# Three forms of the same matrix products in the second layer of a token-mixing MLP

## The chip, the cores and the metric

The kernel runs on one core of one Trainium2 chip. The metric is the device time of one execution in microseconds. Beside plain times there is one profiled execution, in which the hardware profiler records each instruction and each transfer. In its answers PE is TensorE's stream of products, PEld is TensorE's weight loads, DVE is VectorE, ACT is ScalarE, POOL is GpSimd, and SP is the queue that issues most transfers. L1401 means line 1401 of the kernel. A product is written weights' rows * weights' columns, then rows x columns of the streamed operand.

## The reference

The input has 2048 tokens of 448 channels. Two blocks follow each other, each with a layer norm, a scale and shift, and a gate from a small modulation product. The first is a state-space convolution along the tokens. The second, which holds the change, is an MLP along the token axis, shared by all channels:

```
h = layernorm(x) * (1 + cb) + sb              # (2048 tokens, 448 channels)
u = gelu(einsum("bsd,sf->bdf", h, w1) + b1)   # 1792 hidden units per channel
y = einsum("bdf,fs->bds", u, w2) + b2         # back to 2048 tokens
out = x + gb * transpose(y)
```

Everything is float32.

## The kernel before

The first 400 us or so compute the convolution with its Fourier transforms; the change doesn't touch them. They hold products that serve as neighbours of the new forms: line 599 multiplies 64 rows on each half of TensorE's array with 512 streamed columns (type F32R, and bf16), line 802 does so with 224 columns in plain float32, line 1212 uses the whole array with 224 columns in plain float32, and line 682 uses four strips of 32 weight columns with 64 streamed columns.

The MLP works with split operands. Each float32 matrix is held as a high part of the type F32R and a low part that is the remainder (tiles whi and wlo for weights, uh and ul for the hidden units, h3h and h3l for the normed input). One float32 product is made of three: high by high, high weights by low data, low weights by high data.

The first layer (`mlp1`, lines 1325 to 1334) runs over the hidden units in two halves of seven blocks of 128, with seven accumulators in PSUM. `gelu` (line 1369) then writes uh and ul for each half, `kh` = 0 and 1.

The second layer (lines 1390 to 1407) runs over 16 blocks `t` of 128 tokens. For each block it takes one accumulator `o` (128 tokens by 448 channels, one of seven PSUM buffers), and for both halves `kh` and the seven `k` in each it issues the three products of 448 columns, at lines 1401, 1402 and 1403: 42 products a block, 672 in all. The eviction is two operations of VectorE: line 1405 adds the bias and multiplies with the gate, line 1406 adds the residual `xt`, which was loaded back from device memory. Line 1407 stores the block.

The weights come through `WeightStream` (lines 166 to 218). It counts 64 parts of 128 rows by 896 columns; part n = 32 + 2t + kh belongs to half kh of block t. Three buffers take the raw parts from memory (line 190), four hold the split ones. `begin` casts a part to whi on ScalarE (line 207), and `rest` subtracts to wlo on VectorE (line 216) and then issues the load of a later raw part. At the products of part n the kernel calls `ahead(n + 4)`, which makes one part each time, and in the second layer this is part n + 2. A part takes the split buffer of the one four before it, so its cast waits until that one's products are done.

The order of instructions on PE, ACT, DVE and POOL is the order of the program. On SP, in the second layer, a planner sets the order. So on VectorE the two evicting operations of block t stand ahead of the splits that `ahead` issues for block t + 1.

Of the kernel before, what the change touches and what calls it, by code (L numbers as in the profile page):

```python
# [11 lines left out]
F32 = mybir.dt.float32  # L12
# [3 lines left out]
ALU = mybir.AluOpType  # L16
# [5 lines left out]
L, D, N, F = 2048, 448, 256, 1792  # L22
P = 128
# [8 lines left out]
DC = 224  # L32
# [4 lines left out]
WAHEAD = 4  # L37
# [122 lines left out]
def token_pair(a, r, g):  # L160

    rows = a.rearrange("(n g h r) d -> g n h (r d)", g=2, h=2, r=16)
    return rows[g, :, :, r * D : (r + 2) * D]
# [58 lines left out]
def tile_adaln_s4d_mixer(ctx, tc, i, out):  # L222
    nc = tc.nc
# [8 lines left out]
    x2_d = dram.tile([L, D], F32, name="x2_d")  # L232

    cp = ctx.enter_context(tc.tile_pool(name="cp", bufs=1))
    mod = [None] * 3 + [cp.tile([P, D], F32, name=f"mod{k}") for k in range(3, 6)]
# [3 lines left out]
    b2 = cp.tile([P, 16], F32, name="b2")  # L239
# [3 lines left out]
    with ExitStack() as es:  # L243
        V, S, G, T = nc.vector, nc.scalar, nc.gpsimd, nc.tensor
# [47 lines left out]
        xt = xp.tile([P, 16, D], F32, name="xt")  # L292
# [201 lines left out]
        rs = xp.tile([P, 16], F32, name="rs")  # L494
# [455 lines left out]
        rows, cols, pieces = iter(range(16)), iter(range(32)), [0, 0]  # L950
# [88 lines left out]
        for s in range(tail):  # L1039
            if s == 32:  # L1040
# [6 lines left out]
                t0 = fp.tile([P, 2, P], F32, name="t0", bufs=1)  # L1047
# [83 lines left out]
            if s > 32:  # L1131
                go = pieces[0] < NP and (s % 2 == 1 or s >= NHALF)
# [15 lines left out]
        wst = WeightStream(tc, ctx, i)  # L1148
# [18 lines left out]
        def ln_load(r, ahead=True):  # L1167
            vts[r] = rot.tile([P, 2, D], F32, tag="vt", name="vt", bufs=4)
            nc.sync.dma_start(vts[r], v_v[r])
            if ahead and r % 2 and 1 < r < 15:  # L1170
                x_pair(r + 1)
# [26 lines left out]
        def ln_y(r):  # L1198
            y = py.tile([P, D], F32, tag="y", name="y")
            vt = vts.pop(r)  # L1200
            for g in range(2):
                T.matmul(y[64 * g : 64 * g + 64], ft, vt[:, g], start=True, stop=True)  # L1202
            return y_sum(r, y)
# [16 lines left out]
        def ln_mod(r):  # L1220
            mean, rs = sa.pop(r)
            h = rot.tile([P, D], F32, tag="h", name="h", bufs=3)
            total = small("sum", "b")
            V.reciprocal(rs, rs)
            V.scalar_tensor_tensor(h, xts[r // 2][:, r % 2], mean, mod[4], ALU.add, ALU.mult)
            V.scalar_tensor_tensor(h, h, rs, mod[3], ALU.mult, ALU.add, accum_out=total)  # L1226
            sb[r] = stats(h, total, "b")
            hs[r] = h

        def ln_out(r):  # L1230
            mean, rs = sb.pop(r)
            h = hs.pop(r)
            V.reciprocal(rs, rs)
            V.tensor_tensor(mean, mean, rs, ALU.mult)
            if r == 0:

                S.activation(h3h[:, r], h, AF.Identity, bias=mean, scale=rs)  # L1237
                exact = rot.tile([P, D], F32, tag="h", name="h", bufs=3)
                V.tensor_scalar(exact, h, rs, mean, ALU.mult, ALU.add)
                V.tensor_tensor(h3l[:, r], exact, h3h[:, r].bitcast(F32), ALU.subtract)  # L1240
                return None
            S.activation(h, h, AF.Identity, bias=mean, scale=rs)  # L1242
            S.copy(h3h[:, r], h)
            return lambda: V.tensor_tensor(h3l[:, r], h, h3h[:, r].bitcast(F32), ALU.subtract)
# [69 lines left out]
    with ExitStack() as es:  # L1314
        es.enter_context(tc.manual_schedule(engines={ENG.PE, ENG.Activation, ENG.DVE, ENG.Pool}))
        V, S, G = nc.vector, nc.scalar, nc.gpsimd
        kp = es.enter_context(tc.tile_pool(name="mk", bufs=1))
        up = es.enter_context(tc.tile_pool(name="mu", bufs=1))
        pacc = es.enter_context(tc.tile_pool(name="pacc", bufs=7, space=PSUM))
        h3h = kp.tile([P, 16, D], F32R, name="h3h")  # L1320
        h3l = kp.tile([P, 16, D], F32R, name="h3l")
        uh = [up.tile([P, 7, D], F32R, name="uh0"), None]
        ul = [up.tile([P, 7, D], F32R, name="ul0"), None]

        def mlp1(acc, n, f0=0, f1=7):
            fh, r = divmod(n, 16)
            hi, lo = wst.parts[n]
            if f1 == 7:
                wst.parts.pop(n)
            for f in range(f0, f1):  # L1330
                fs = slice(f * P, (f + 1) * P)
                nc.tensor.matmul(acc[f], hi[:, fs], h3h[:, r], start=r == 0, stop=False)  # L1332
                nc.tensor.matmul(acc[f], hi[:, fs], h3l[:, r], start=False, stop=False)  # L1333
                nc.tensor.matmul(acc[f], lo[:, fs], h3h[:, r], start=False, stop=r == 15)  # L1334

        first = ExitStack()
        first.enter_context(tc.manual_schedule(engines={ENG.SP}))
        acc = [pacc.tile([P, D], F32, tag="acc", name="acc") for _ in range(7)]
        for t in range(-2, 16):

            part = wst.begin(t + WAHEAD - 1) if t > 0 else None
            last = ln_out(t + 1) if 0 <= t + 1 < 16 else None

            if t == -1:
                second()
            if t == 0:
                part = wst.begin(3)
                mlp1(acc, 0, 0, 4)
                ln_y(3)()
            if t == -1 or 0 < t < 13:  # L1350
                ln_y(t + 3)()
            if 4 <= t + 7 < 16:
                ln_load(t + 7)
            if t < 0:
                wst.load()
            if 1 <= t + 2 < 16:
                ln_mod(t + 2)
            if last:
                last()
            wst.rest(part, V)  # L1360
            if t == 0:
                mlp1(acc, 0, 4, 7)
            elif t > 0:
                mlp1(acc, t)
        first.close()
        e3.close()
        ru = es.enter_context(tc.tile_pool(name="m2r", bufs=3))

        def gelu(acc, fh):
            for f in range(7):  # L1370
                k = 7 * fh + f
                u = ru.tile([P, D], F32, tag="u", name="u")
                S.activation(u, acc[f], AF.Gelu_apprx_tanh, bias=b1[:, k : k + 1])
                V.tensor_copy(uh[fh][:, f], u)
                V.tensor_tensor(ul[fh][:, f], u, uh[fh][:, f].bitcast(F32), ALU.subtract)

        gelu(acc, 0)
        acc = [pacc.tile([P, D], F32, tag="acc", name="acc") for _ in range(7)]
        for r in range(16):
            if r < 8:  # L1380
                for g in range(2):
                    rows = xts[r][64 * g : 64 * g + 64].rearrange("p r d -> p (r d)")
                    nc.sync.dma_start(token_pair(x2_d, 2 * r, g), rows)
            wst.ahead(16 + r + WAHEAD, V)
            mlp1(acc, 16 + r)
        e2.close()
        uh[1] = up.tile([P, 7, D], F32R, name="uh1")
        ul[1] = up.tile([P, 7, D], F32R, name="ul1")
        gelu(acc, 1)
        for t in range(16):  # L1390
            ss = slice(t * P, (t + 1) * P)
            xt = ru.tile([P, D], F32, tag="x2", name="x2")
            nc.sync.dma_start(xt, x2_d[ss])
            o = pacc.tile([P, D], F32, tag="acc", name="o")
            for kh in range(2):
                n = 32 + 2 * t + kh
                wst.ahead(n + WAHEAD, V)
                hi, lo = wst.parts.pop(n)
                for k in range(7):
                    ks = slice(k * P, (k + 1) * P)  # L1400
                    nc.tensor.matmul(o, hi[:, ks], uh[kh][:, k], start=kh == 0 and k == 0, stop=False)  # L1401
                    nc.tensor.matmul(o, hi[:, ks], ul[kh][:, k], start=False, stop=False)  # L1402
                    nc.tensor.matmul(o, lo[:, ks], uh[kh][:, k], start=False, stop=kh == 1 and k == 6)  # L1403
            y = ru.tile([P, D], F32, tag="y", name="y")
            V.scalar_tensor_tensor(y, o, b2[:, t : t + 1], mod[5], ALU.add, ALU.mult)  # L1405
            V.tensor_tensor(y, y, xt, ALU.add)  # L1406
            nc.sync.dma_start(out[0, ss], y)


# [25 lines left out]
```

## Time and profile before

| what | us |
|---|---|
| median of three runs | 693.96 |
| the three runs | 693.78, 693.96, 703.75 |
| profiled execution, device time | 697.46 |
| its span, first to last instruction | 695.5 |
| second layer, first weight load to last product | 556.3 to 690.7 |

The span is 2 us shorter than the device time of the same execution. The page lists busy time of each engine, the chain of work that ended last, the costliest groups of instructions, and the transfers. Products on TensorE overlap: a record's length is how long one product is under way, and the distance between two starts is what each costs in a stream. The mean granted clock of TensorE was 0.961 over the span, and 1.00 in the second layer. Each plain float32 product of the program leaves two records of a product and of a weight load; each F32R product leaves one.

### The profile page before, as it was taken

To read this page: it belongs to the slowest core of one execution; us is meant where nothing else is said; L and a number is where in the kernel's file an instruction comes from. 1 tells how busy PE (TensorE), PEld (TensorE's weight loads), DVE (VectorE), ACT (ScalarE), POOL (GpSimd) and SP (SyncE) were. 2 spreads that over 40 slices of the span, in tenths; PEclk is the share of its full clock that TensorE was granted. 3 is DMA by queue.
4 is the path that set the end of the run, shared out by engine and by line. 5 is a ranking of instruction groups with operands and counts; after the bars stand their busy time and mean duration, and the time that the engine had idled before them with its cause. 6 is when DMAs were issued, how large, how long until landed. Compare 5 with 4: busy or idle time off the path is not lost. (4 is left out here: it accounts for less than half of the span.)

```text
span 695.5 us, 18257 instructions
## 1 busy us (share of the span) xinstructions
PE 621.8 (89%) x7180; PEld 462.8 (67%) x7180; DVE 459.1 (66%) x880; ACT 438.2 (63%) x876; POOL 270.8 (39%) x324
## 2 busy tenths in 40 slices
PE   0759888888988889798889989999999999999997
PEld 0335455545535556565567767778999999999996
DVE  7469899779879679585886578776622354444431
ACT  5937698878978899999964568777422332222220
POOL 6496548429639778988876300000000000000000
PEclk9988979899999899899999999999999999999999
DMA  7795565357896535545348899975673445555640
GB/s 175 203 198 128 176 218 162 120 200 243 252 293 218 169 98 136 152 119 151 90 117 244 270 245 260 245 177 142 178 237 109 144 132 159 159 159 168 167 130 27
DMA packets 103987, 121.14 MB, mean 174 GB/s; under 512 B 12858, under 2 KB 91822, under 8 KB 103774
## 3 DMA queue, kind: packets, MB, share of 16 engines
q1 hardware_dynamic: 102366, 113.11, 56.6%
q0 software_dynamic: 1536, 6.87, 4.6%
q8 instruction: 57, 0.93, 0.6%
q14 instruction: 28, 0.23, 0.1%
HBM read 84.59 MB, written 34.87 MB: 172 GB/s over the span
## 5 line engine op out<-in xcount | busy, mean ns | idle before, releaser
L207 ACT CAST whi<-w 128x896 fp32r<-128x896 f32 x64 | 59.8, 939 | 133.2 <-PE o L1402 84.7
L651 POOL TENSOR_TENSOR G<-mag,gs 128x512 f32<-128x512 f32 x56 | 71.9, 1283 | 75.7 <-ACT gs L647 75.5
L216 DVE TENSOR_TENSOR wlo<-w,whi 128x896 fp32r<-128x896 f32 x64 | 68.0, 1086 | 40.3 <-ACT whi L207 31.0
L1332 PE MATMUL acc<-h3h,whi 128*128 128x448 f32 x224 | 83.4, 373 | 0.9 <-ACT h3h L1237 0.9
L599 PE MATMUL xg<-tab,lph 64*128 64x512 f32 x112 | 65.5, 587 | 19.8 <-issue 7.1
L1333 PE MATMUL acc<-h3l,whi 128*128 128x448 f32 x224 | 82.2, 367 | 0.0
L682 PEld LDWEIGHTS kg<-E,G 128*32 128x32 f32 x3584 | 60.3, 120 | 32.6 <-issue 15.9
L1402 PE MATMUL o<-ul,whi 128*128 128x448 f32 x224 | 81.4, 363 | 0.0
L1401 PE MATMUL o<-uh,whi 128*128 128x448 f32 x224 | 81.2, 363 | 0.0
L1334 PE MATMUL acc<-h3h,wlo 128*128 128x448 f32 x224 | 81.2, 362 | 0.0
L1403 PE MATMUL o<-uh,wlo 128*128 128x448 f32 x224 | 80.7, 360 | 0.0
L682 PE MATMUL kg<-E,G 128*32 128x64 f32 x3584 | 70.5, 236 | 4.3 <-issue 3.5
L599 PE MATMUL xe<-tab,lph 64*128 64x512 f32 x112 | 65.7, 590 | 8.7 <-ACT gs L648 7.0
L652 POOL TENSOR_TENSOR G<-mag,gs 128x512 f32<-128x512 f32 x56 | 71.8, 1282 | 0.0
L1405 DVE SCALAR_TENSOR_TENSOR y<-o,b,mod 128x448 f32<-128x448 f32 x16 | 10.9, 684 | 80.3 <-PE o L1403 80.3
L628 POOL TENSOR_TENSOR m<-mag,w 128x512 f32<-128x512 f32 x56 | 60.3, 1077 | 6.0 <-DVE E L659 1.5
L653 DVE TENSOR_TENSOR E<-m,xe 128x512 f32<-128x512 f32 x56 | 38.1, 681 | 27.2 <-ACT xe L646 23.5
L636 ACT ACTIVATE ab<-xe 128x512 f32<-128x512 f32 x56 | 33.9, 606 | 30.6 <-PE xe L599 22.9
L1332 PEld LDWEIGHTS acc<-h3h,whi 128*128 128x128 f32 x224 | 42.4, 189 | 14.0 <-ACT h L1242 4.2
L599 PE MATMUL xe<-tab,lex 64*128 64x512 f32 x56 | 31.9, 579 | 18.5 <-DMA lex<-wm 16.9
L610 ACT ACTIVATE mag<-xe 128x512 f32<-128x512 f32 x56 | 35.6, 636 | 14.3 <-PE xe L599 5.4
L1334 PEld LDWEIGHTS acc<-h3h,wlo 128*128 128x128 f32 x224 | 42.4, 189 | 3.1
(236 smaller groups left out, 1472.5 us busy)
## 6 DMA issues: line engine op xcount, KB each, us to landing
w<-in_B_w_dram SPq DMA_DIRECT2D x64, 224.0 KB
w<-in_B_w_dram SPq DMA_DIRECT2D x32, 448.0 KB
yu_d<-yt SPq DMA_DIRECT2D x16, 448.0 KB
yi<-yu_d SPq DMA_DIRECT2D x16, 448.0 KB
us_d<-uo SPq DMA_DIRECT2D x16, 448.0 KB
u<-us_d SPq DMA_DIRECT2D x32, 224.0 KB
v_d<-vt SPq DMA_DIRECT2D x32, 224.0 KB
vt<-v_d SPq DMA_DIRECT2D x14, 448.0 KB
```

Source lines behind the costliest of these rows:

```text
L216: eng.tensor_tensor(lo, w, hi.bitcast(F32), ALU.subtract)
L599: T.matmul(out[k], lhs[r], rhs[r], start=start, stop=stop)
L628: G.tensor_tensor(m2, me, w[:, :, None].to_broadcast([P, GD, 32]), ALU.mult)
L651: G.tensor_tensor(Gt[:, 1], mg_, v32(sg), ALU.mult)
L652: G.tensor_tensor(Gt[:, 0], mg_, v32(cg_), ALU.mult)
L682: T.matmul(kgs[g][32 * q : 32 * q + 32, m], Gt[:, c, d], E[:, c, d], start=h == 0 and c == 0 and m == 0, stop=h == 1 and c == 1, skip_grou ...
L1332: nc.tensor.matmul(acc[f], hi[:, fs], h3h[:, r], start=r == 0, stop=False)
L1333: nc.tensor.matmul(acc[f], hi[:, fs], h3l[:, r], start=False, stop=False)
L1334: nc.tensor.matmul(acc[f], lo[:, fs], h3h[:, r], start=False, stop=r == 15)
L1401: nc.tensor.matmul(o, hi[:, ks], uh[kh][:, k], start=kh == 0 and k == 0, stop=False)
L1402: nc.tensor.matmul(o, hi[:, ks], ul[kh][:, k], start=False, stop=False)
L1403: nc.tensor.matmul(o, lo[:, ks], uh[kh][:, k], start=False, stop=kh == 1 and k == 6)
```

## The change

The 16 token blocks no longer have one form. Blocks 2 and 3 split each product into two of 224 columns with the same weights, in two accumulators. Blocks 4 and 5 split each into two of 64 rows, one on each half of the array, with an accumulator for each half; the eviction adds the two. Blocks 10 and 11 are computed together: their four parts of weights are made first, and then the products of the two blocks alternate, each in its own accumulator. The other ten blocks are as before. The arithmetic is that of before; with halves of 64 rows the order of the sums differs.

```diff
-        for t in range(16):
-            ss = slice(t * P, (t + 1) * P)
-            xt = ru.tile([P, D], F32, tag="x2", name="x2")
-            nc.sync.dma_start(xt, x2_d[ss])
-            o = pacc.tile([P, D], F32, tag="acc", name="o")
-            for kh in range(2):
-                n = 32 + 2 * t + kh
-                wst.ahead(n + WAHEAD, V)
-                hi, lo = wst.parts.pop(n)
-                for k in range(7):
-                    ks = slice(k * P, (k + 1) * P)
-                    nc.tensor.matmul(o, hi[:, ks], uh[kh][:, k], start=kh == 0 and k == 0, stop=False)
-                    nc.tensor.matmul(o, hi[:, ks], ul[kh][:, k], start=False, stop=False)
-                    nc.tensor.matmul(o, lo[:, ks], uh[kh][:, k], start=False, stop=kh == 1 and k == 6)
-            y = ru.tile([P, D], F32, tag="y", name="y")
-            V.scalar_tensor_tensor(y, o, b2[:, t : t + 1], mod[5], ALU.add, ALU.mult)
-            V.tensor_tensor(y, y, xt, ALU.add)
-            nc.sync.dma_start(out[0, ss], y)
+        def mlp2(n, t, products):
+            wst.ahead(n + WAHEAD, V)
+            hi, lo = wst.parts.pop(n)
+            kh = n % 2
+            for k in range(7):
+                ks = slice(k * P, (k + 1) * P)
+                first_, last_ = kh == 0 and k == 0, kh == 1 and k == 6
+                products(hi[:, ks], uh[kh][:, k], first_, False)
+                products(hi[:, ks], ul[kh][:, k], False, False)
+                products(lo[:, ks], uh[kh][:, k], False, last_)
+
+        def whole(o):
+            return lambda w, u, start, stop: nc.tensor.matmul(o, w, u, start=start, stop=stop)
+
+        def column_halves(o):
+            def go(w, u, start, stop):
+                for c in range(2):
+                    cs = slice(c * DC, c * DC + DC)
+                    nc.tensor.matmul(o[c][:, 0:DC], w, u[:, cs], start=start, stop=stop)
+
+            return go
+
+        def row_halves(o):
+            def go(w, u, start, stop):
+                for c in range(2):
+                    rs = slice(64 * c, 64 * c + 64)
+                    nc.tensor.matmul(o[c], w[rs], u[rs], start=start, stop=stop)
+
+            return go
+
+        forms = {2: "columns", 3: "columns", 4: "rows", 5: "rows"}
+        for t0 in range(16):
+            if t0 == 11:
+                continue
+            both = (10, 11) if t0 == 10 else (t0,)
+            os_, xs_ = [], []
+            form = forms.get(t0)
+            for t in both:
+                xt = ru.tile([P, D], F32, tag="x2", name="x2")
+                nc.sync.dma_start(xt, x2_d[t * P : (t + 1) * P])
+                xs_.append(xt)
+                count = 2 if form in ("columns", "rows") else 1
+                os_.append([pacc.tile([P, D], F32, tag="acc", name="o") for _ in range(count)])
+            if t0 == 10:
+                parts = []
+                for n in range(32 + 2 * t0, 36 + 2 * t0):
+                    wst.ahead(n + WAHEAD, V)
+                    parts.append(wst.parts.pop(n))
+                for kh in range(2):
+                    for k in range(7):
+                        ks = slice(k * P, (k + 1) * P)
+                        for term in range(3):
+                            for j in range(2):
+                                w = parts[2 * j + kh][term == 2]
+                                u = (uh, ul, uh)[term][kh]
+                                nc.tensor.matmul(
+                                    os_[j][0], w[:, ks], u[:, k],
+                                    start=kh == k == term == 0, stop=kh == 1 and k == 6 and term == 2,
+                                )
+            else:
+                o = os_[0]
+                how = (
+                    column_halves(o) if form == "columns" else row_halves(o) if form == "rows"
+                    else whole(o[0])
+                )
+                for n in (32 + 2 * t0, 33 + 2 * t0):
+                    mlp2(n, t0, how)
+            for t, o, xt in zip(both, os_, xs_):
+                y = ru.tile([P, D], F32, tag="y", name="y")
+                bias, gate = b2[:, t : t + 1], mod[5]
+                if form == "columns":
+                    for c in range(2):
+                        cs = slice(c * DC, c * DC + DC)
+                        V.scalar_tensor_tensor(y[:, cs], o[c][:, 0:DC], bias, gate[:, cs], ALU.add, ALU.mult)
+                elif form == "rows":
+                    V.tensor_scalar(y, o[0], bias, None, ALU.add)
+                    V.tensor_tensor(y, y, o[1], ALU.add)
+                    V.tensor_tensor(y, y, gate, ALU.mult)
+                else:
+                    V.scalar_tensor_tensor(y, o[0], bias, gate, ALU.add, ALU.mult)
+                V.tensor_tensor(y, y, xt, ALU.add)
+                nc.sync.dma_start(out[0, t * P : (t + 1) * P], y)
```

## The prediction

> **What bounds the kernel now.** I read the page first (engines, chain), then the stretch of the second layer by itself, then single products in order of time.
>
> ```profile
> span 695.5 us, 18257 instructions
> ...
> PE 621.8 (89%) x7180; PEld 462.8 (67%) x7180; DVE 459.1 (66%) x880; ACT 438.2 (63%) x876; POOL 270.8 (39%) x324
> ...
> PE acc L1332 7%; PE acc L1333 7%; PE o L1402 7%; PE o L1401 6%; PE acc L1334 6%; PE o L1403 6%; PE y L1202 2%; ACT whi L207 0%; ACT sq L1188 0%; ACT L1291 0%; ACT h3h L1237 0%; DVE h L1226 0%; DVE y L1405 0%; DVE y L1406 0%; ACT rs L1189 0%
> ```
>
> The last stage of the chain is TensorE alone: L1401 to L1403 are the second layer's products. The next answer is the table by stretches, cut to the tile o (window, length; busy time and count of PE, PEld, DVE; clock; DMA share; GB/s). Below it stand the two kinds of record of L1401 (min/median/max ns).
>
> ```profile
> 556.30:690.70 134.40, 134.22 (x672) 125.99 (x672) 10.26 (x15) 1.00 0.50 141
> ```
>
> ```profile
> L1401 PEld LDWEIGHTS o<-uh,whi x224: 187/188/188, 556.3 to 690.1; 128*128 128x128 f32 x112
> L1401 PE MATMUL o<-uh,whi x224: 362/363/363, 556.5 to 690.3; 128*128 128x448 f32 x112
> ...
> L1402 PEld LDWEIGHTS o<-ul,whi x224: 187/188/188, 556.5 to 690.3; 128*128 128x128 f32 x112
> ```
>
> 134.40 / 672 = 0.200 us from product to product, at a clock of 1.00, with no idle time: 16 blocks of 42 products, 8.40 us each. The 363 ns are a latency; products overlap. L1401 and L1402 use the same weights one after the other, and each has its own weight load, so a product split in two will load twice. Whatever a block's products cost more or less lands in the time in full. The change touches six blocks, 50.4 us of TensorE. To be 2% faster (13.9 us; 2% is about what a measurement of this kernel can tell from no change) these would have to shrink by 28%.
>
> **Blocks 2 and 3, 224 columns: 84 products each in place of 42.** What spaces narrow products, streaming or the weight load? No product of the type F32R under 448 columns is in the trace, so I bound it. First the start of a stage of the first layer, where TensorE had stood still and the first load is in the open:
>
> ```profile
> 429.91 0.48 PE L1332 MATMUL acc<-h3h,whi 128*128 128x448 f32 x1
> 430.23 0.36 PE L1333 MATMUL acc<-h3l,whi 128*128 128x448 f32 x1
> 430.43 0.36 PE L1334 MATMUL acc<-h3h,wlo 128*128 128x448 f32 x1
> ```
>
> ```profile
> 429.91 0.19 PEld L1332 LDWEIGHTS acc<-h3h,whi 128*128 128x128 f32 x1 [0.70 <-ACT whi L207]
> 430.02 0.19 PEld L1333 LDWEIGHTS acc<-h3l,whi 128*128 128x128 f32 x1
> 430.23 0.19 PEld L1334 LDWEIGHTS acc<-h3h,wlo 128*128 128x128 f32 x1
> ```
>
> The first product is 0.12 longer than the others (0.48 against 0.36), and the second starts 0.32 after the first: 0.12 from load to streaming, and 0.20 of product. The second load starts 0.11 after the first, the third when the second product starts (430.23). So a load runs behind the product before it, keeps the load path for 0.11, and lets its product begin 0.12 after it starts; the 0.19 of its record is latency. Streaming 224 columns takes half of 0.20 at most, 0.10. The load is longer, so the spacing becomes 0.12: 84 × 0.12 = 10.1 us against 8.4, +1.7 a block, **+3.4 us** for two. Bounds: 0.11 (the loads' distance) gives 9.2, +1.7 for two; 0.13 (load to streaming, if the product itself were 0.19 of the 0.32) gives 10.9, +5.0.
>
> The Trainium skill, "TensorE: Matmul & The Clock Gate", section "Back-to-back issue gap", gives columns / 2.4 + 2.5 ns for an isolated warm product: 95.8 ns at 224 columns, an estimate of 8.05 us a block and −0.7 us for two. For 448 columns it gives 189 ns, where the trace has 200; the page itself says that it leaves out the load's budget at small sizes.
>
> Blocks 2 and 3 evict with two operations of 224 columns for one of 448; at worst each costs as much as one now (0.68, row below). DVE then waits 5 us a block for TensorE, which covers it; without that cover it would be 0.7 a block.
>
> **Blocks 4 and 5, 64 rows on both halves: 42 pairs each.** Two neighbours: pairs of plain f32 products on 64 rows and 224 columns (L802; the program's product gives two records, so four are two pairs), and F32R pairs of 512 columns (L599).
>
> ```profile
> 376.84 0.55 PE L802 MATMUL vv<-z,bt 64*128 64x224 f32 x4
> 377.22 0.55 PE L802 MATMUL vv<-z,yk 64*128 64x224 f32 x4
> 377.59 0.55 PE L802 MATMUL vv<-z,bt 64*128 64x224 f32 x4
> ```
>
> ```profile
> 203.11 0.50 PE L599 MATMUL xe<-tab,lph 64*128 64x512 f32 x1
> 203.11 0.50 PE L599 MATMUL xg<-tab,lph 64*128 64x512 f32 x1
> 203.46 0.39 PE L599 MATMUL xe<-ones,mg 64*128 64x512 bf16 x1
> ```
>
> L802: two pairs in 0.375, 0.19 a pair, two loads included: the halves load and stream side by side. L599: both halves start together; 0.35 to the next, less 0.12 for the open load, is 0.23 for 512 columns, so 0.20 for 448. I take 0.20, **0 us**; the other end is 0.19, −0.4 a block, −0.9 for two. Entering and leaving the halved form costs something: at L1212 (whole array) to L802 (halves)
>
> ```profile
> 392.11 1.78 PE L1212 MATMUL y<-vt,fl 128*128 128x224 f32 x8
> 393.82 0.65 PE L802 MATMUL vv<-z,yk 64*128 64x224 f32 x4
> 394.31 0.55 PE L802 MATMUL vv<-z,bt 64*128 64x224 f32 x4
> ```
>
> ```profile
> L1212 PE MATMUL y<-vt,fl x32: 352/353/458, 392.1 to 402.1; 128*128 128x224 f32 x32
> ```
>
> the last of eight starts at 393.89 − 0.35 = 393.54. One of these takes (1.78 − 0.46)/7 = 0.19, so the next was due at 393.73 and came 0.09 late; the first four then take 0.49 instead of 0.375. That is 0.2 a switch, **+0.4** for two. The eviction grows from two DVE operations to four, +1.3 us by the row of L1406 below: behind it on DVE stand the splits of the weights (L216), needed 8.4 us later, and seven PSUM buffers leave three blocks before one is wanted again. Free; else 1.3 a block.
>
> **Blocks 10 and 11, taking turns: 84 products of the same form.** At 0.200 they cost nothing by themselves; if the 0.01 over f32's 0.19 came from writing one accumulator in a row, −0.9. What is new is when weights are wanted. Around the start of block 10:
>
> ```profile
> 640.28 0.36 PE L1403 MATMUL o<-uh,wlo 128*128 128x448 f32 x1
> 640.48 0.36 PE L1401 MATMUL o<-uh,whi 128*128 128x448 f32 x1
> ```
>
> ```profile
> 640.68 0.68 DVE L1405 SCALAR_TENSOR_TENSOR y<-o,b,mod 128x448 f32<-128x448 f32 x1 [5.05 <-PE o L1403]
> 641.40 0.63 DVE L1406 TENSOR_TENSOR y<-y,x 128x448 f32<-128x448 f32 x1
> 641.94 2.08 DVE L216 TENSOR_TENSOR wlo<-w,whi 128x896 fp32r<-128x896 f32 x2
> ```
>
> The two operations of L216 split parts 54 and 55, block 11's. They stand in DVE's order behind the eviction of block 9, and the first is done at 641.94 + 1.04 = 642.98. Today part 54 is wanted at 648.88. Taking turns, the sixth product wants its wlo: 640.48 + 5 × 0.20 = 641.48. TensorE waits 1.5, then sees a load in the open (0.12) and the signal (about 0.1): **+1.7 us**, a new wait on VectorE; everything on PE is queued behind it. Bounds +0.8 (with the −0.9) and +2.0. Parts 56 and 57 take the buffers of 52 and 53 (four buffers), so ACT's cast of 56 waits for the middle of the pair and that of 57 for its end, some 8.4 and 4 us ahead of their use; cast 0.94 and split 1.04 fit. DVE then has split 57, two evictions (2.6) and split 58, about 5.5 us, and 58 is wanted 8.4 after the pair. SP's weight loads behind these splits slip by the same few us, with over 8 us to go. Free.
>
> The end does not change: block 15 keeps its form.
>
> **Sum.** 3.4 + 0 + 0.4 + 1.7 = +5.5 us. The profiled execution took 697.46 us (span 695.5), so it would take 703.0; it lies 3.5 above the median of 693.96. On the median the sum gives **699.5 us**. The bounds: 1.7 − 0.9 + 0.4 + 0.8 = +2.0, or 0 if the split comes earlier than I place it; 5.0 + 0 + 0.4 + 2.0 = +7.4. This case's own range is 694 to 702, within 2%. Chance 0.69.
>
> **Rivals.** *Narrow F32R products run like plain f32* (slower). L1212 is plain f32, 128 rows and 224 columns: 16 products in the program are 32 records, 0.19 apart, so 0.38 for one. Should the one-record form hold only for wide products, blocks 2 and 3 cost 84 × 0.38 = 31.9 us, +23.5 each; with +0.4 and +1.7, 49.1 and 743.1 us. It decides wherever the width goes under its limit. Against: nothing in the trace ties the type to a width. For: nothing denies it, since every F32R product here has 448 or 512 columns. Chance 0.17. The Trainium skill, "FP8 and Floating Point Precision", section "TensorE Precision Notes", has four passes for true FP32 and a truncated reading for the reduced form, with no word of a width; the two records of L1212 fit its first half.
>
> *The weight load does not hide behind a narrow product of the same rows* (slower). Then a product costs 0.10 + 0.12 = 0.22: 84 × 0.22 = 18.5, +10.1 each, +20.2 + 2.1 = 22.3: 716.3; if the spacing were the load's record plus a gap, 0.20 whatever the width, +16.8 + 2.1: 712.9. The Trainium skill, "TensorE: Matmul & The Clock Gate", section "The mechanism", says that loads overlap products in flight only where their row groups differ; by that, the 448-column products too would be spaced by more than 0.20. Against the rival is also the smallest product:
>
> ```profile
> L682 PEld LDWEIGHTS kg<-E,G x3584: 105/110/178, 36.5 to 359.9; 128*32 128x32 f32 x200
> ```
>
> ```profile
> 340.90 1.10 PE L682 MATMUL kg<-E,G 128*32 128x64 f32 x64
> ```
>
> 16 rounds on the four column tiles in 1.10, under 0.07 a round, while a load's record lasts 0.11: its latency is hidden there. Chance 0.07.
>
> *The halves take turns instead of running side by side* (slower): 84 × 0.20 = 16.8, +16.8 for two; with 3.4 + 0.4 + 1.7, 22.3: 716.3. L599 and L802 speak against it. Chance 0.05.
>
> *Faster by over 2%*: no row gives it; 0.02.
>
> **Chances and range.** Faster 0.02; within 2% 0.69; slower 0.17 + 0.07 + 0.05 = 0.29. The range must leave out no more than 0.2: it takes in the first case, the loads and the halves, 694 to 717, and leaves out plain f32 and faster (0.19).
>
> **What would show it.** In the changed trace: 224-column products 0.12 apart with one record each (0.38 or two records: plain f32; 0.20 or more: the load); halves in pairs starting together, 0.20 apart; one wait of about 1.7 us on wlo at the sixth product of the pair, and no other idle time of PE; blocks 6 to 9 and 12 to 15 still 8.4 us. I am wrong if the narrow spacing leaves 0.11 to 0.13, or if PE waits anywhere after the pair.

## The result and the profile after

The changed kernel takes 1.0059 times as long as the kernel before, with a 95% interval of 1.0035 to 1.0083: on a median of 696.84 us that is +4.1 us, between +2.4 and +5.8. The median of its 18 runs is 701.63 us. The prediction was +5.5, within 2%, and 699.5 us. It had counted from the median of three runs, 693.96; 18 runs put the kernel before at 696.84, and +5.5 on that is 702.3. That 699.5 lies within 2.1 us of the measured median is therefore partly luck: the starting point was 2.9 too low, and the sum was too high.

One profiled execution of it has a span of 701.8 us, against 695.5. Of these 6.3 us only 4.1 lie in the second layer. The other 2.2 lie ahead of it, where the programs are the same; in the profiled executions below the second layer begins anywhere from 553.8 to 559.4 us. So I read the second layer alone.

The page of the changed kernel, engines and chain:

```profile
PE 624.1 (89%) x7348; PEld 464.7 (66%) x7348; DVE 461.4 (66%) x886; ACT 437.7 (62%) x876; POOL 270.4 (39%) x324
...
PE 7%; DVE 0%; issue 0%
PE o L1402 5%; PE o L1445 2%; DVE y L1469 0%; DVE y L1470 0%
```

168 products have been added. The chain of TensorE's work, which took in the whole MLP before, now goes back only through 7% of the span, some 50 us. There TensorE had stopped, in the pair of blocks 10 and 11 (L1445).

The table by stretches of the changed kernel, cut to the tile o, has one row for each form (window, length; busy time and count of PE, PEld and DVE; clock; DMA share; GB/s):

```profile
558.67:575.47 16.80, 16.80 (x84) 15.75 (x84) 0.68 (x1) 1.00 0.49 137
575.47:594.32 18.85, 18.85 (x171) 18.73 (x169) 1.50 (x4) 1.00 0.53 148
594.32:611.32 17.00, 17.00 (x170) 15.63 (x169) 2.11 (x4) 1.00 0.54 155
611.32:645.03 33.71, 33.71 (x170) 31.60 (x169) 3.36 (x5) 1.00 0.59 168
645.03:663.55 18.52, 17.09 (x86) 15.67 (x85) 0.68 (x2) 1.00 0.45 125
663.55:697.15 33.60, 33.60 (x169) 31.31 (x167) 3.41 (x5) 1.00 0.33 96
sum 138.48, PE 137.05 PEld 128.69 DVE 11.74; mean PE 22.84 PEld 21.45 DVE 1.96
```

In order: blocks 0 and 1, whole; 2 and 3, 224 columns; 4 and 5, halves; 6 to 9, whole; 10 and 11, taking turns; 12 to 15, whole. Each row runs from the first start in its blocks to the first start behind them, the last one to 0.20 behind its last start. Two plain blocks took 16.80 before and do so here. The narrow blocks take 18.85 (+2.05), the halves 17.00 (+0.20), the four blocks behind them 33.71 (+0.11), the pair 18.52 (+1.72), and the rest is as before. The sum is 138.48 against 134.40: +4.08 us, which is what the timed runs show. The weight loads are busy for 18.73 of 18.85 us in the row of the narrow blocks and for 15.75 of 16.80 in that of the plain ones. This alone doesn't say that the loads are the limit: a load's record is 0.19 long, so records that start 0.11 apart overlap and always look busy. In the row of the pair PE is busy for 17.09 of 18.52: a hole of 1.43 in the records.

Narrow products, halves and the switch from one to the other, in order of time (start, length of the group in us):

```profile
594.00 0.38 PE L1408 MATMUL o<-uh,wlo 128*128 128x224 f32 x2
594.32 0.47 PE L1416 MATMUL o<-uh,whi 64*128 64x448 f32 x2
594.63 0.36 PE L1416 MATMUL o<-ul,whi 64*128 64x448 f32 x2
594.83 0.36 PE L1416 MATMUL o<-uh,wlo 64*128 64x448 f32 x2
```

Each group of L1416 is one pair of halves: its two products fit in the length of one, 0.36, and pairs follow at 0.20. The first pair is 0.11 longer: its load starts together with the pair instead of ahead of it, so the load isn't hidden. Two narrow products take 0.22 from start to start; here, at the switch, 0.32. The way out looks the same:

```profile
611.03 0.36 PE L1416 MATMUL o<-uh,wlo 64*128 64x448 f32 x2
611.32 0.48 PE L1402 MATMUL o<-uh,whi 128*128 128x448 f32 x1
611.63 0.36 PE L1402 MATMUL o<-ul,whi 128*128 128x448 f32 x1
```

The steps are 0.29 and 0.31 in place of 0.20 and 0.20. So a switch costs about 0.2 us, half before it and half behind, and the two switches together 0.4. Half of the first switch (0.09) lies in the row of the narrow blocks, so 224 columns cost 18.85 − 16.80 − 0.09 = 1.96 us. The row of the halves holds the other half (0.11) and half of the second switch (0.09), so the halves themselves cost 17.00 − 16.80 − 0.11 − 0.09 = 0.

The start of the pair, on PE and on VectorE:

```profile
645.03 0.56 PE L1445 MATMUL o<-uh,whi 128*128 128x448 f32 x2
645.43 0.56 PE L1445 MATMUL o<-ul,whi 128*128 128x448 f32 x2
645.83 0.37 PE L1445 MATMUL o<-uh,wlo 128*128 128x448 f32 x1
647.63 0.47 PE L1445 MATMUL o<-uh,wlo 128*128 128x448 f32 x1 [1.43 <-DVE wlo L216]
```

```profile
645.23 0.68 DVE L1469 SCALAR_TENSOR_TENSOR y<-o,b,mod 128x448 f32<-128x448 f32 x1 [5.05 <-PE o L1402]
645.95 0.62 DVE L1470 TENSOR_TENSOR y<-y,x 128x448 f32<-128x448 f32 x1
646.49 2.08 DVE L216 TENSOR_TENSOR wlo<-w,whi 128x896 fp32r<-128x896 f32 x2
```

Five products run, and the sixth, the first with the second block's wlo, starts 1.80 after the fifth instead of 0.20: 1.6 of waiting. Its load isn't hidden either, which makes it 0.11 longer (0.47 against 0.36). On VectorE the split that it wants is the first of the two at L216. It starts only when both evicting operations are through, at 646.49, and its record is 1.085 long, so it ends at 647.58.

### The profile page after: what moved, and what is told of

Same layout as the page of the kernel before. It is cut to its first block, busy times and chain, and to the rows that moved or that the text cites. A ratio compares the mean times of both kernels' runs of the same rounds, so it can differ in the third digit from the quotient of the medians.

```text
span 701.8 us, 18600 instructions
## 1 busy us (share of the span) xinstructions
PE 624.1 (89%) x7348; PEld 464.7 (66%) x7348; DVE 461.4 (66%) x886; ACT 437.7 (62%) x876; POOL 270.4 (39%) x324
## 5 line engine op out<-in xcount | busy, mean ns | idle before, releaser
L216 DVE TENSOR_TENSOR wlo<-w,whi 128x896 fp32r<-128x896 f32 x64 | 68.0, 1086 | 47.4 <-ACT whi L207 38.1
L599 PE MATMUL xe<-tab,lph 64*128 64x512 f32 x112 | 65.7, 589 | 10.4 <-ACT gs L648 8.0
L1402 PE MATMUL o<-uh,whi 128*128 128x448 f32 x140 | 50.9, 363 | 0.0
L1402 PE MATMUL o<-ul,whi 128*128 128x448 f32 x140 | 50.8, 363 | 0.0
L1402 PE MATMUL o<-uh,wlo 128*128 128x448 f32 x140 | 50.4, 360 | 0.0
L610 ACT ACTIVATE mag<-xe 128x512 f32<-128x512 f32 x56 | 35.5, 634 | 16.4 <-PE xe L599 5.0
L1333 PEld LDWEIGHTS acc<-h3l,whi 128*128 128x128 f32 x224 | 42.4, 189 | 2.7 <-DVE h3l L1240 0.5
```

What stands on the lines that cost most here:

```text
L216: eng.tensor_tensor(lo, w, hi.bitcast(F32), ALU.subtract)
L599: T.matmul(out[k], lhs[r], rhs[r], start=start, stop=stop)
L1402: return lambda w, u, start, stop: nc.tensor.matmul(o, w, u, start=start, stop=stop)
```

## The experiments

My theory after the result was that the narrow blocks pay for weight loads, that the halves pay nothing but the switch, and that the pair pays for a place in VectorE's order. Its rivals were that the narrow cost belongs to something else (a fixed cost of each product, or the place of those two blocks), that the evictions are not covered, and that the hole comes from buffers or transfers. The code cuts below are shortened. The kernels with other widths, with other types and with narrow products alone ran once each, so only the rows of that one execution are read.

### The split earlier, all else as changed

```diff
                 for n in range(32 + 2 * t0, 36 + 2 * t0):
-                    wst.ahead(n + WAHEAD, V)
+                    if n > 52:
+                        wst.ahead(n + WAHEAD, V)
 ...
+                if t0 == 9:
+                    wst.ahead(56, V)      # behind block 9's products, ahead of its eviction
```

> The changed kernel with one move: the split of part 54 stands ahead of the eviction of block 9 on VectorE instead of behind it; everything else stays. If VectorE's order makes the 1.8 us hole at the sixth product of blocks 10 and 11, the hole goes: 84 products in 16.8 us instead of 18.5, the second layer 136.8 us instead of 138.5, about 1.0035 times the kernel before. If the four split buffers or the transfers of the raw weights make it, the hole stays (18.5 us), or comes back at the middle or behind the pair.

The table by stretches of this kernel, first the pair, then the whole layer:

```profile
640.12:656.92 16.80, 16.80 (x86) 15.76 (x84) 0.68 (x1) 1.00 0.44 126
553.76:690.52 136.76, 136.76 (x840) 128.88 (x839) 11.74 (x19) 1.00 0.48 138
```

16.80 us for 84 products: the hole is gone and nothing came in its place, in the middle or behind. VectorE shows the split in the time in which it had waited for TensorE:

```profile
636.89 1.09 DVE L216 TENSOR_TENSOR wlo<-w,whi 128x896 fp32r<-128x896 f32 x1 [1.62 <-ACT whi L207]
640.32 0.68 DVE L1472 SCALAR_TENSOR_TENSOR y<-o,b,mod 128x448 f32<-128x448 f32 x1 [2.34 <-PE o L1402]
```

The layer takes 136.76 us, +2.36 over the kernel before, where 136.8 was expected. The time is 1.0027 times that of before, with an interval of 0.9996 to 1.0057, so the timed runs can't tell it from no change, and the reading rests on the stage. The edit moves the whole call, the cast on ACT and the next load with it, but the cast has not moved: it starts 4.20 us ahead of the pair in both kernels (640.83 before 645.03, and 635.92 before 640.12). So it is the split's place on VectorE that made the 1.7 us. Taking turns between two accumulators is worth nothing either way: 16.80 / 84 = 0.200 us a product.

### Every block by 224 columns

```diff
-        forms = {2: "columns", 3: "columns", 4: "rows", 5: "rows"}
+        forms = {t: "columns" for t in range(16)}      # and no pair
```

> All 16 blocks by products of 224 columns, no halves, no turns. If a narrow product costs 0.113 us wherever it stands and nothing hides it, each block takes 9.4 us instead of 8.4: the second layer 150.8 us, +16.4, about 1.024 times the kernel before. If the cost came from the two blocks' place (a start-up, evictions, weights late), most blocks go back to 8.4 and the sum stays under +5.

```profile
554.47:704.63 150.16, 150.16 (x1344) 150.04 (x1343) 12.14 (x31) 1.00 0.45 126
```

150.16 / 1344 = 0.1117 us a product. The layer is 15.8 us longer, near the 16.4 expected. The time is 1.0225 times that of before (1.0169 to 1.0280): slower, though not surely by 2%. The cost goes with the number of products, not with the place.

### Every block by halves

```diff
-        forms = {2: "columns", 3: "columns", 4: "rows", 5: "rows"}
+        forms = {t: "rows" for t in range(16)}         # and no pair
```

> All 16 blocks by products of 64 rows on both halves, no narrow products, no turns. If the halves run side by side at 0.202 us a pair, each block takes 8.5 us, the way in costs 0.1 once, and the four-operation eviction shows only behind the last block, about 1.3 us: in all about +2.9 us, 1.004 times the kernel before. If the longer evictions were not covered, idle time of TensorE shows at the block borders, up to 1.3 us a block, +20 us.

```profile
556.72:691.24 134.52, 134.52 (x1344) 125.93 (x1344) 19.59 (x30) 1.00 0.50 141
```

134.52 us against 134.40: nearly all of the 0.12 is the half of the switch that lies in this row (0.11), and 672 pairs cost what 672 whole products cost. I had put 0.202 a pair into the expectation, from blocks that held a switch; the row gives 0.200. The time of VectorE's operations that read `o` nearly doubles (19.59 us against 10.26), and PE is busy throughout, so the longer eviction is covered in 15 of 16 blocks. Behind the last block it shows:

```profile
691.44 0.68 DVE L1463 TENSOR_SCALAR y<-o,b 128x448 f32<-128x448 f32 x1 [5.67 <-PE o L1416]
692.23 0.62 DVE L1464 TENSOR_TENSOR y<-y,o 128x448 f32<-128x448 f32 x1
692.88 0.62 DVE L1465 TENSOR_TENSOR y<-y,mod 128x448 f32<-128x448 f32 x1
693.54 0.62 DVE L1468 TENSOR_TENSOR y<-y,x 128x448 f32<-128x448 f32 x1
```

It is 2.75 us to the store at 694.19. Two operations take 1.37 in the kernel before, from 691.08 to its store at 692.45. The ratio is 1.0017 (0.9986 to 1.0048), where 1.004 was expected; the interval holds both that and no change.

### Other widths

```diff
+            2: cols=(112,) * 4,        4: cols=(152, 148, 148),   6: cols=(256, 192),
+            8: cols=(320, 128),       10: cols=(384, 64),        12: cols=(64,) * 7,
+        # for n in cols: matmul(o[:, c0 : c0 + n], w, u[:, c0 : c0 + n], ...)
```

> The loop of before, with six blocks cut into other widths, all in one accumulator: block 2 four of 112 columns, block 4 152 + 148 + 148, block 6 256 + 192, block 8 320 + 128, block 10 384 + 64, block 12 seven of 64. Theory: a narrow F32R product is spaced by the weight load, 0.113 us whatever its width, and a wide one by its columns, 0.2 us x columns / 448. That gives 18.9, 14.2, 9.8, 10.9, 12.0 and 33.2 us for these blocks. Rival: a product costs its columns plus a fixed 0.02 us. That gives 11.1, 10.4, 9.2, 9.2, 9.2 and 13.5 us. The plain blocks between stay at 8.4.

One row for each of the blocks 2, 4, 6, 8 and 10, here with all instructions in the stretch, so that ACT and POOL stand behind DVE:

```profile
576.18:594.88 18.70, 18.70 (x169) 18.70 (x168) 3.31 (x4) 2.13 (x3) 0.00 (x0) 1.00 0.28 75
603.34:617.37 14.03, 14.03 (x127) 14.02 (x126) 3.31 (x4) 2.02 (x3) 0.00 (x0) 1.00 0.36 99
625.82:635.41 9.59, 9.59 (x85) 9.59 (x84) 3.32 (x4) 1.91 (x3) 0.00 (x0) 1.00 0.52 145
643.84:654.61 10.77, 10.77 (x85) 10.77 (x84) 3.31 (x4) 1.94 (x3) 0.00 (x0) 1.00 0.46 129
663.07:675.03 11.96, 11.96 (x86) 11.95 (x84) 3.32 (x4) 1.97 (x3) 0.00 (x0) 1.00 0.41 116
```

The theory gave 18.9, 14.2, 9.8, 10.9 and 12.0; the rival gave 11.1, 10.4 and 9.2 three times. Products of 112 columns and of about 150 cost 0.111 each (18.70/168 and 14.03/126), as those of 224 do. So each product has a floor, whatever its width below that of the floor. The rival, a cost in proportion to the columns plus a constant, is off by 7.6 us in the first block alone.

Block 12 missed both numbers: it took 57.9 us, where the theory gave 33.2 and the rival 13.5. The kernel took 775.75 us. That is the subject of the last section.

### Other types, and halves of 224

```diff
+            2: cols=(224, 224),                       4: cols=(448,), as bf16,
+            6: cols=(224, 224), as bf16,              8: cols=(112,) * 4, as bf16,
+           10: cols=(224, 224), 64 rows on each half, 12: cols=(224, 224), as plain float32,
```

> The loop of before, with six blocks in other forms, all but block 10 in one accumulator. Block 2: two of 224 columns, F32R. Block 4: whole products of 448 columns whose operands are the upper halves of the same words read as bf16 (this leaves out the lower bits in blocks 4, 6 and 8, so their sums are coarse). Block 6: two of 224 in bf16. Block 8: four of 112 in bf16. Block 10: 64 rows on both halves and 224 columns, F32R. Block 12: two of 224 in plain float32. Theory: the F32R weight load spaces narrow products at 0.112 us; a bf16 load is shorter (its record is 0.09 us in the first stage against 0.19), so bf16 products are spaced by their columns alone. That gives 9.4 us for block 2, 7.9 to 8.4 for blocks 4, 6 and 8, 9.4 for block 10 (84 pairs at 0.112), and 84 x 0.38 = 31.8 for block 12, the price of the rival that narrow products run like plain float32. Rival: a narrow product has a fixed cost of its own, whatever its type. Then blocks 6 and 8 take 9.4 and more, like their F32R forms (9.4 and 18.7).

```profile
575.11:584.48 9.37, 9.37 (x85) 9.37 (x84) 0.68 (x1) 1.00 0.53 149
592.91:601.06 8.15, 8.15 (x43) 0.02 (x1) 0.68 (x1) 1.00 0.61 171
609.66:618.00 8.34, 8.34 (x86) 0.03 (x1) 0.68 (x1) 1.00 0.59 167
626.50:635.07 8.57, 8.57 (x169) 0.02 (x1) 0.68 (x1) 1.00 0.60 161
643.66:653.22 9.56, 9.56 (x169) 9.45 (x168) 0.68 (x1) 1.00 0.52 146
661.74:693.35 31.61, 31.61 (x169) 31.61 (x168) 0.68 (x1) 1.00 0.17 46
```

The records of the weight loads of both types:

```profile
L1430 PEld LDWEIGHTS <-whi x196: 96/97/102, 592.9 to 634.8; 128*128 128x128 bf16 x196
L1430 PEld LDWEIGHTS o<-uh,whi x140: 182/190/192, 574.9 to 691.6; 128*128 128x128 f32 x84, 64*128 64x128 f32 x56
```

The first row here is block 2, then come blocks 4, 6, 8, 10 and 12. The 8.15 of block 4 is a little short, since the record of the product behind it starts 0.03 after the block's last one. With the upper halves of the same words, the same widths and a shorter load, the narrow block falls from 9.37 us to 8.34 (block 6), 0.099 a product. Four products of 112 take 8.57 (block 8), just above the 8.4 expected; that is 0.051 a product, where F32R takes 18.70. So the floor belongs to the type F32R and is no fixed cost of every product. That it is the load of this type, and not its product, rests on one more row: at 429.91 and 430.02 in the prediction's lines two F32R loads start 0.11 apart, and TensorE had stood still before them. No run made the F32R load shorter and left its product as it was, so this last step is argued.

Halves with 224 columns (block 10) cost 9.56 us, of which about 0.2 is the two halves of switches in that row: the loads of two halves run side by side, but each half has the same floor. One accumulator for both narrow products (block 2) makes no difference against two. Plain float32 costs 31.61 us: that is what the first rival of the prediction would have meant, 31.9 there.

## Why the prediction was right

*What bounds.* This was right: TensorE bounds the stage, and each term landed in the time in full. It is +4.08 us in the stage and +4.1 in the timed runs.

*224 columns, +3.4.* The mechanism, a spacing by the weight load, was right, and the size was off: 1.96 us were measured. The term that was mis-sized is the spacing of 0.12 us, which is 0.1117. The 0.12 is the time from a load to its product, read twice as a difference of rows that are rounded to 0.01 (0.48 − 0.36 and 0.32 − 0.20). The same records in ns give less (min/median/max, from 429.8 to 441 us in the kernel before):

```profile
L1332 PE MATMUL acc<-h3h,whi x15: 362/363/476, 429.9 to 440.5; 128*128 128x448 f32 x15
```

The product with the open load is 476 − 363 = 113 ns longer. At 0.113 the same sum gives 84 × 0.113 = 9.5 us a block and +2.2 for two, and at the measured 0.1117 it gives +1.96. So rounding made most of the error. The distance of two loads (430.02 − 429.91 = 0.11), which the prediction took as its lower bound, gave +1.7. With 0.113 and 0.1117 so close, the runs don't tell whether a load follows the load before it or waits for the product before it to start.

The Trainium skill, "TensorE: Matmul & The Clock Gate", section "Back-to-back issue gap", has a formula for isolated products that gives 95.8 ns at 224 columns, an estimate. Both types are above it in this stream: F32R at 0.1117 us, and bf16, without the load's floor, at 0.099.

*Halves, 0, and switches, +0.4.* Both were right: 0.200 a pair, and 0.4 for two switches. That the four-operation eviction is covered was right too. The 1.3 us that the prediction names as the price without the cover is near the 1.4 that it costs behind the last block when that block has the form.

*Taking turns, +1.7.* This was right: +1.72, at the sixth product, from the split behind the eviction of block 9, and moving the split took it away. Two small errors cancel in it. The split ends 1.085 us after its start, not 1.04, which is the distance to the next one; and the signal, which the prediction put at about 0.1 with no row for it, took about 0.05 (from 647.58 to the start of the load at 647.63). What I took to be free behind the pair was free: blocks 12 to 15 take 33.60.

*The rivals.* Narrow F32R products don't run like plain float32: they leave one record each, 0.112 apart, where plain float32 leaves two and takes 0.38 in all. The weight load does hide behind a narrow product of the same rows, up to the spacing of 0.112; the rival asked for 0.20 or more. The halves do run side by side. And wide products don't come nearer to 0.19 by taking turns, so the lower bound that counted on this was idle.

The sum came out 1.4 us too high, all of it in the one term.

## What to carry to other kernels

A split product pays for each weight load again: under the width that covers the load (for F32R here 0.1117 us, or 250 columns at 0.446 ns each) the cost is the number of products, whatever their columns. When work is interleaved, look at which operand is now wanted first and where its producer stands in the order of its engine; here the wait was cured by moving one call. Read a stream's price from the distance of starts. If it has to come from a small difference, take the records in ns: an error of 0.007 us, 168 times over, is 1.2 us.

## What the runs showed of the hardware that was not expected

*TensorE's clock falls under a stream without gaps, if the products are narrow.* Here are the rows of block 12 in the kernel with other widths (seven products of 64 columns in place of one), its first 2.5 us and the rest, and then the plain block behind it in two parts:

```profile
683.51:686.00 2.49, 2.49 (x25) 2.48 (x23) 2.25 (x4) 0.94 (x1) 0.00 (x0) 1.00 0.01 5
686.00:741.37 55.37, 55.37 (x273) 55.37 (x273) 1.06 (x2) 1.88 (x2) 0.00 (x0) 0.52 0.09 26
741.37:745.50 4.13, 4.13 (x12) 3.70 (x13) 3.31 (x4) 0.00 (x0) 0.00 (x0) 0.50 0.36 114
745.50:752.35 6.85, 6.85 (x32) 6.34 (x32) 0.00 (x0) 0.94 (x1) 0.00 (x0) 0.91 0.22 65
```

PE is busy by its records for all of it, and the granted clock is 0.52. The plain block behind takes 10.98 us in place of 8.40, so it loses some 2.6 us until the clock is back. A run was made to see whether it is the width:

```diff
+            2: cols=(90, 90, 90, 90, 88),   5: cols=(76, 76, 74, 74, 74, 74),   8: cols=(64,) * 7,
```

> The loop of before, with three blocks of narrow F32R products in one accumulator: block 2 five of 88 to 90 columns, block 5 six of 74 or 76, block 8 seven of 64. Each is spaced by the weight load at 0.111 us, so the columns stream for 33%, 28% and 24% of the time. Theory: the granted clock falls by half, as in the block of seven 64s of the run before, when the share of streaming falls under some bound between 42% (112 columns, clock 1.00) and 24% (64 columns, 0.52), although products follow without a gap. At 1.00 the blocks take 23.4, 28.1 and 32.8 us; each one under the bound takes 2.5 us at that rate and then twice as long, with 4 us of the next block at half clock. Rival: the fall came from something else in that run, such as the late weights around block 12; then block 8 keeps its clock.

```profile
571.45:577.00 5.55, 5.55 (x52) 5.54 (x50) 0.68 (x1) 1.00 0.54 154
577.00:610.58 33.58, 33.58 (x162) 33.58 (x162) 0.00 (x0) 0.51 0.06 17
629.56:635.00 5.44, 5.44 (x51) 5.43 (x49) 0.69 (x1) 1.00 0.52 153
635.00:677.73 42.73, 42.73 (x206) 42.73 (x205) 0.00 (x0) 0.51 0.05 14
697.22:700.20 2.98, 2.98 (x29) 2.97 (x27) 0.68 (x1) 1.00 0.18 69
700.20:756.91 56.71, 56.71 (x270) 56.71 (x269) 0.00 (x0) 0.50 0.08 22
```

There are two rows for each of the blocks 2, 5 and 8, cut where the clock falls. All three blocks fall to half, after 3 to 6 us, and their products then stand nearly twice as far apart: seven of them take 1.49 us, from 721.07 to 722.56, or 0.213 each in place of 0.112. So it was not the place. The bound lies between 112 columns in 0.111 us, which kept a clock of 1.00 for 18.70 us, and 90 columns, which did not; with 0.446 ns a column that is between 45% and 36% of the time spent streaming. I did not narrow it further. That the share of streaming decides is my reading: it goes with the width here, and no run separates the two. The 224 columns of the change, at 89%, are far from the bound. The Trainium skill, "TensorE: Matmul & The Clock Gate", section "What's actually happening", has a half-rate state for an idle engine; the 0.50 agrees with that state, but here no product waited and the records show no idle time.

*A column costs about 0.44 ns in F32R, and in bf16 read from every second half-word, but less in plain float32, as far as it can be read.* For F32R it is 0.200 / 448 = 0.446. Strided bf16 is 0.198 from start to start within block 4, or 0.442. The narrow products of block 6 are 0.099 by their row and 0.100 by their starts (609.65 to 617.97 for 83 steps), or 0.44 to 0.45. For plain float32 it is 31.61 us / 168 records / 448 = 0.420, if each of the two records of a product streams its 224 columns twice; no run shows that it does. On this reading, the 0.011 us by which a whole F32R product is longer than the prediction's plain float32 neighbour is paid by the column. It does not belong to the load, since bf16 with its shorter load costs nearly as much as F32R, nor to the accumulator, since taking turns left 0.200. What makes it was not tested.
